# Attention packed into an FFN, one core: batch 0's FFN half tiles leave PSUM by a ScalarE copy, and |h| is made from the copy on VectorE

## The chip, the cores and the metric

The kernel runs on one core of a Trainium2 chip. A core has five engines that work in parallel, each through its own instructions in order: TensorE (PE; its weight loads are listed as PEld), VectorE (DVE), ScalarE (ACT), GpSimd (POOL) and SyncE (SP, which only issues DMAs here). The metric is the device time of one execution in microseconds. Before the change it is 772.9 us, the median of three runs (772.86, 772.90, 773.84).

## The reference: what is computed

Two softmax attentions in a row (32 packed queries `p` attend to `k`, `v`; the 576 queries `q` then attend to the 32 packed results), for 8 batches of 8 heads, followed by a two-layer FFN whose activation is softplus, written in its stable form:

```python
p_packed = sm_attn(p, k, v)
out = sm_attn(q, p_packed, p_packed)
x = out.transpose(0, 2, 1, 3).reshape(B * S, H * D)     # 4608 x 512
h = x @ w_in                                            # 4608 x 2048
g = np.maximum(h, 0.0) + np.log1p(np.exp(-np.abs(h)))
return (g @ w_out).astype(np.float32)                   # 4608 x 512
```

The two FFN weights arrive as 64-bit floats. The kernel turns them into 32-bit values itself, 128 columns (or rows) at a time.

## The kernel before

**FFN units.** A batch's hidden layer is cut along the 2048 hidden features into 16 blocks of 128. A unit is one pair (batch b, block f), so there are 128 units, u = 16 b + f. `gemm1` (line 581) computes the unit's h, transposed, 128 features by 576 rows, as two half tiles of 288 columns, named `ph`, each in a PSUM bank of its own; each takes six matmuls, since every factor is split in a high and a low part (`at_h`, `at_l`, `mh`, `ml`) and three products are summed. The pool of `ph` has two buffers (`ps_h`, bufs=2), so the two halves of unit u occupy both of them, and `gemm1` of unit u+1 can write a half only when the last reader of that half of unit u is through.

**Softplus** (lines 598 to 615, a generator whose parts are emitted between the tiles of the second GEMM). ScalarE writes |h| from `ph` into an SBUF tile `e` (line 603). For batch 0 the Exp and Ln (lines 605, 606) run once over all 576 columns, after both halves; for later batches once per half. VectorE then adds max(h, 0), which it reads from `ph` once more (line 608, one instruction per half): this is the last reader of `ph`. Then GpSimd saves the last 64 columns in `rest` (line 612), and VectorE splits the first 512 into `gh` and `gl` (lines 595, 596).

**The second GEMM** (line 619) runs LAG = 2 units behind: PE's order in a step is gemm1(u), then four tiles of gemm2(u-2), with pieces of the next batch's attention between those tiles, and after every second unit of batch 0 the matmuls of `make_m` (line 544), which multiply the packed attention into a piece of `w_in` that the unit two steps on needs.

**What else runs in batch 0's stage.** The weights are converted while batch 0's units run: a DMA brings 64-bit words into `x` (two buffers, and two places in `rest` at first), ScalarE makes `m` and `r` from them (lines 200, 204), VectorE masks and shifts (lines 206, 211), GpSimd adds (line 219); for `w_out` ScalarE and VectorE split the result in `wo_h` and `wo_l` (lines 238, 244). Batch 1's attention runs there too: its transposes and scores go through the two `ps_m` banks, which ScalarE empties (lines 269, 285, 310, 559).

**What sets the order.** PE's order is the program's own. For the other engines a planner orders the instructions beforehand by priority, with its own costs; on the chip each engine then works through its list in order and waits at an instruction whose inputs are not there.

**Names the change uses.** `aT` is a tag with two buffers: the attention output of a batch, read last by `weights(b)` (lines 526, 527), which makes `at_h` and `at_l` before the batch's first unit. `a1` is a tag with two buffers: the first scores of a batch, last read by the transposes of line 309.

Of the kernel before, what the change touches and what calls it, by code (L numbers as in the profile page):

```python
# [9 lines left out]
F32 = mybir.dt.float32  # L10
F32R = mybir.dt.float32r
AF = mybir.ActivationFunctionType
ALU = mybir.AluOpType
AX = mybir.AxisListType
I32 = mybir.dt.int32
# [11 lines left out]
def pack_attention_then_softplus_ffn(  # L27
# [10 lines left out]
    nc = tc.nc  # L38
    B, H, S, D = q.shape
    J = p.shape[2]  # L40
    DM, DFF = w_in.shape
    P = 128
# [3 lines left out]
    C = S // 2  # L46
# [9 lines left out]
    scale = 1.0 / math.sqrt(D)  # L56
# [4 lines left out]
    work = ctx.enter_context(tc.tile_pool(name="work", bufs=2))  # L61
# [15 lines left out]
    def rest_at(b, f):  # L77

        return f + NF if f < LAG and b // 2 % 2 else f
# [37 lines left out]
    def load(nm, b, g):  # L117
        if b >= B:
            return
        src = {"q": q, "k": k, "v": v}[nm][b, g * HG:(g + 1) * HG]  # L120
        if b < FIRST:
            if (nm, b) == ("q", 0):
                o = DFF - (g + 1) * SI * D
                t = w_in_sb[:NP, :, o:o + SI * D].rearrange("x h (s d) -> x h s d", d=D)
            else:
                t = ld.tile([NP, HG, SI, D], F32, tag="ld", name=f"{nm}_{b}_{g}")
            nc.sync.dma_start(
                t.rearrange("x h s d -> x h (s d)"),
                src.rearrange("h (x s) d -> x h (s d)", s=SI),
            )  # L130
        elif nm == "v":
            t = ld.tile([NP, HG, SI, D], F32, tag="ld", name=f"{nm}_{b}_{g}")
            nc.sync.dma_start(
                t.rearrange("x h (m c) d -> x (h m) (c d)", c=2),
                src.rearrange("h (m x c) d -> x (h m) (c d)", x=NP, c=2),
            )
        else:
            t = ld.tile([P, HG, C], F32, tag="ld", name=f"{nm}_{b}_{g}")
            by_quad = src.rearrange("h (n x c) (e d) -> c e x (h n) d", x=Q, c=2, d=Q)
            for i in range(P // Q):  # L140
                nc.sync.dma_start(
                    t[i * Q:(i + 1) * Q].rearrange("x h (n d) -> x (h n) d", d=Q),
                    by_quad[i // 2, i % 2],
                )
        loaded[nm, b, g] = t
# [390 lines left out]
    def make_m(b, c, res):  # L536


        n = m_cols(b)
        pss = [bank(f"psm_{b}_{c}_{g}") for g in range(G)]  # L540
        for g, ps in enumerate(pss):
            for hh in range(HG):
                o = D * g
                nc.tensor.matmul(  # L544
                    ps[hh * J:(hh + 1) * J, :n],
                    res["pt"][g][o:o + D, hh * J:(hh + 1) * J],
                    w_in_sb[o:o + D, hh, c * n:(c + 1) * n],
                    start=True, stop=True,
                )
        pool, th, tl = (cv, "t", "r") if b and c % 2 == 0 else (work, "mh", "ml")  # L550
        halves = []
        for g, ps in enumerate(pss):
            o = g * n % MC
            if o == 0:
                mh = pool.tile([P, MC], F32R, tag=th, name=f"mh_{b}_{c}_{g}", bufs=2)
                ml = pool.tile([P, MC], F32R, tag=tl, name=f"ml_{b}_{c}_{g}", bufs=2)
                halves.append((mh, ml))
            cols = slice(o, o + n)
            nc.scalar.copy(mh[:, cols], ps[:, :n])  # L559
            nc.vector.tensor_tensor(  # L560
                ml[:, cols], ps[:, :n], mh[:, cols].bitcast(F32), op=ALU.subtract
            )
        res["m"][c] = halves
# [24 lines left out]
    def halves(nm):  # L588
        return [
            work.tile([P, NT * P], F32R, tag=t, name=f"{t}_{nm}", bufs=LAG + 1)  # L590
            for t in ("gh", "gl")
        ]

    def split(hi, lo, x):
        nc.vector.tensor_copy(hi, x)  # L595
        nc.vector.tensor_tensor(lo, x, hi.bitcast(F32), op=ALU.subtract)  # L596

    def softplus(b, f, hv, done):
        e = work.tile([P, S], F32, tag="e", name=f"e_{b}_{f}")
        es = [e[:, c * C:(c + 1) * C] for c in range(2)]  # L600
        spans = [e] if b == 0 else es
        for c in range(2):
            nc.scalar.activation(es[c], hv[c], AF.Abs)  # L603
            for x in spans[c:c + 1] if b else spans[:c]:
                nc.scalar.activation(x, x, AF.Exp, scale=-1.0)  # L605
                nc.scalar.activation(x, x, AF.Ln, bias=1.0)  # L606
        for c in range(2):
            nc.vector.scalar_tensor_tensor(es[c], hv[c], 0.0, es[c], op0=ALU.max, op1=ALU.add)  # L608
        yield
        yield  # L610
        r = (b % 2) * REST
        nc.gpsimd.tensor_copy(rest[:, rest_at(b, f), r:r + REST], e[:, NT * P:])  # L612
        yield
        done[b, f] = halves(f"{b}_{f}")
        split(*done[b, f], e[:, :NT * P])
# [58 lines left out]
        order.append(("o", f))  # L674
    PACE = 0.56
    FRONT = 1000
    PACE_FIRST = 0.62
    CONV = 1.6
    CONV_EARLY = 1.6
# [18 lines left out]
    for st in range(NF * NT):  # L698
        with tc.high_priority(offset=FRONT):
            if next(steps, steps) is steps:  # L700
# [5 lines left out]
    for nm in ("k", "v"):  # L706
        for g in range(G):
            load(nm, 1, g)
    with tc.high_priority(offset=FRONT):
        make_m(0, 0, res[0])  # L710
# [7 lines left out]
    for u in range(len(units) + LAG):  # L718
        if u < len(units):
            b, f = units[u]  # L720
            if f == 0:
                if (b + 1) % BG == 0 and b + 1 < B:
                    pack_transposed((b + 1) // BG, pt)
                ahead = attention(b + 1) if b + 1 < B else iter(())
                due = 0.0
            chain = softplus(b, f, gemm1(b, f, res[b]), gs)
            next(chain)
            if f == NF - 1:
                if (b + 2) % BG == 0 and b + 2 < B:
                    pt = load_pack((b + 2) // BG, (nc.sync,))  # L730
                for _ in ahead:
                    pass
                if b + 1 < B:
                    weights(b + 1)
# [9 lines left out]
        for t in range(NT):  # L744
# [6 lines left out]
            if u < len(units):  # L751
                due += PACE if b != FIRST - 1 else PACE_FIRST
                while due >= 1:
# [10 lines left out]
        if u + 2 < len(units):  # L764


            nb, c = units[u + 2][0], units[u + 2][1] * P
# [31 lines left out]
```

## Time and profile before

| | before |
|---|---|
| median of three runs | 772.9 us |
| profiled execution, its own time | 772.78 us |
| its span (first to last instruction) | 771.0 us |
| mean granted TensorE clock | 0.973 |
| busy over the span: PE, DVE, ACT, POOL | 733.0, 527.6, 434.8, 99.1 us |

The profile is one execution. The execution's own time is 1.8 us more than its span. A row of a timeline gives start, duration, engine, line, operation, tiles and shape; in brackets stands how long the engine had been idle before it, and which instruction ended that. A row of waits gives who waited for what: the sum in us, how often, the longest. A row of a group ends in its busy time, the mean of one instruction in ns, and the idle time before them. A row of the chain of waits gives start, duration and what was on the path. The span is not alike all over: PE waits in its first 150 us and hardly anywhere after them.

### The profile page before, as it was taken

The page shows a single profiled execution, that of the slowest core. Times are in us where ns is not written, and L with a number is a line of the kernel's source. Part 1 is how long each engine was busy: PE and PEld are TensorE (multiplying, and loading weights), DVE is VectorE, ACT ScalarE, POOL GpSimd, SP SyncE. Part 2 cuts the span into 40 slices and gives each one's busy share as a digit, 9 for nine tenths or more (in the row PEclk, how much of TensorE's full clock was granted, in tenths as well). Part 3 has the DMA queues.
Part 4 walks back from the last instruction along what each step waited for, and adds up shares of the span by engine and source line. Part 5 has one row for each costly group of instructions (what it writes and reads, how often), then busy time and mean ns, then how long its engine had stood idle before and what let it go on. Part 6 is the DMA issues. An engine that isn't in the chain of part 4 may idle for free.

```text
span 771.0 us, 14168 instructions
## 1 busy us (share of the span) xinstructions
PE 733.0 (95%) x5360; PEld 579.5 (75%) x5360; DVE 527.6 (68%) x1092; ACT 434.8 (56%) x1057; POOL 99.1 (13%) x166
## 2 busy tenths in 40 slices
PE   6657998999999999999999999999999999999997
PEld 3445775887787778878788777878787777888886
DVE  2697879965877569565967559575867558565554
ACT  5668877766454545565555455565555355555540
POOL 1143444200000000000000000000010000000110
PEclk9559999999999999999999999999999999999999
DMA  9978655434403341052302342052402400010002
GB/s 211 237 185 190 185 137 150 95 76 73 93 1 76 56 81 44 1 124 47 79 1 76 55 64 61 1 109 42 91 2 61 70 1 1 1 55 1 1 1 68
DMA packets 149668, 55.97 MB, mean 73 GB/s; under 512 B 116320, under 2 KB 142944, under 8 KB 149600
## 3 DMA queue, kind: packets, MB, share of 16 engines
q1 hardware_dynamic: 149328, 55.00, 31.9%
q8 instruction: 42, 0.69, 0.4%
q14 instruction: 26, 0.21, 0.1%
q10 hardware_dynamic: 272, 0.07, 0.0%
HBM read 45.61 MB, written 9.44 MB: 71 GB/s over the span
## 4 chain that ended last, share of the span: by engine, by line
PE 85%; DVE 6%; ACT 4%; DMA 3%; issue 1%; POOL 1%; SPq 0%; ACTq 0%; DVEq 0%; POOLq 0%
PE acc L619 42%; PE ph L581 26%; PE acc_m L619 6%; PE psm L544 4%; PE ps L276 2%; DMA w_in_sb<-in_q 2%; PE psp L319 2%; PE psa L309 1%; DVE at_l L527 1%; DVE e L608 1%; DVE t L206 1%; ACT e L605 1%; DVE t L211 1%; ACT e L603 1%; DMA k<-in_k 1%
## 5 line engine op out<-in xcount | busy, mean ns | idle before, releaser
L603 ACT ACTIVATE e<-ph 128x288 f32<-128x288 f32 x256 | 103.2, 404 | 190.4 <-PE ph L581 143.4
L619 PE MATMUL acc<-wo_h,gh 128*128 128x512 f32 x512 | 208.0, 406 | 0.0
L608 DVE SCALAR_TENSOR_TENSOR e<-ph,e 128x288 f32<-128x288 f32 x256 | 113.4, 451 | 132.4 <-ACT e L606 131.3
L619 PE MATMUL acc<-wo_l,gh 128*128 128x512 f32 x512 | 201.2, 393 | 0.0
L619 PE MATMUL acc<-wo_h,gl 128*128 128x512 f32 x512 | 201.0, 393 | 0.0
L581 PE MATMUL ph<-at_h,mh 128*128 128x288 f32 x512 | 159.0, 311 | 12.7 <-ACT at_h L526 6.6
L581 PE MATMUL ph<-at_l,mh 128*128 128x288 f32 x512 | 153.6, 300 | 3.7 <-DVE at_l L527 3.7
L581 PE MATMUL ph<-at_h,ml 128*128 128x288 f32 x512 | 152.9, 299 | 0.0
L581 PEld LDWEIGHTS ph<-at_h,mh 128*128 128x128 f32 x512 | 97.9, 191 | 46.7 <-DVE gl L596 9.6
L612 POOL COPY rest<-e 128x64 f32<-128x64 f32 x128 | 53.8, 420 | 577.3 <-DVE e L608 547.7
L619 PEld LDWEIGHTS acc<-wo_h,gh 128*128 128x128 f32 x512 | 96.4, 188 | 27.5 <-issue 10.2
L619 PEld LDWEIGHTS acc<-wo_h,gl 128*128 128x128 f32 x512 | 96.3, 188 | 21.1
L605 ACT ACTIVATE e<-e 128x288 f32<-128x288 f32 (+1 forms) x240 | 109.4, 456 | 4.0
L606 ACT ACTIVATE e<-e 128x288 f32<-128x288 f32 (+1 forms) x240 | 109.4, 456 | 3.2
L619 PEld LDWEIGHTS acc<-wo_l,gh 128*128 128x128 f32 x512 | 96.6, 189 | 13.1
L581 PEld LDWEIGHTS ph<-at_l,mh 128*128 128x128 f32 x512 | 98.1, 192 | 8.1 <-DVE at_l L527 5.3
L581 PEld LDWEIGHTS ph<-at_h,ml 128*128 128x128 f32 x512 | 98.1, 192 | 0.0
L596 DVE TENSOR_TENSOR gl<-e,gh 128x512 fp32r<-128x512 f32 x128 | 87.7, 685 | 5.5
L559 ACT CAST mh<-psm 128x512 fp32r<-128x512 f32 (+1 forms) x72 | 35.9, 539 | 54.5 <-PE psm L544 54.3
L595 DVE CAST gh<-e 128x512 fp32r<-128x512 f32 x128 | 55.5, 434 | 5.5 <-DVE e L608 0.5
L560 DVE TENSOR_TENSOR ml<-psm,mh 128x512 fp32r<-128x512 f32 (+1 forms) x72 | 42.8, 623 | 20.6 <-ACT mh L559 20.0
L544 PE MATMUL psm<-w_in_sb,pt 64*32 64x512 f32 (+1 forms) x576 | 41.3, 567 | 7.6 <-ACT T_k L269 4.8
(79 smaller groups left out, 696.4 us busy)
## 6 DMA issues: line engine op xcount, KB each, us to landing
v<-in_v SPq DMA_DIRECT2D x16, 576.0 KB, 4.9
x_i<-in_moe_w_in SPq DMA_DIRECT2D x28, 256.0 KB, 4.4
k<-in_k SPq DMA_DIRECT2D x48, 144.0 KB, 3.2
q<-in_q SPq DMA_DIRECT2D x48, 144.0 KB, 3.1
x_o<-in_moe_w_out SPq DMA_DIRECT2D x11, 512.0 KB, 3.8
out<-o SPq DMA_DIRECT2D x18, 256.0 KB, 2.5
rest<-in_moe_w_out SPq DMA_DIRECT2D x5, 512.0 KB, 6.1
k<-in_k SPq DMA_DIRECT2D x4, 576.0 KB, 6.7
```

The source lines that it names most:

```text
L544: nc.tensor.matmul(ps[hh * J:(hh + 1) * J, :n], res["pt"][g][o:o + D, hh * J:(hh + 1) * J], w_in_sb[o:o + D, hh, c * n:(c + 1) * n], start ...
L559: nc.scalar.copy(mh[:, cols], ps[:, :n])
L560: nc.vector.tensor_tensor(ml[:, cols], ps[:, :n], mh[:, cols].bitcast(F32), op=ALU.subtract)
L581: nc.tensor.matmul(ph[:, :C], x[:, ms], y[:, g, cs], start=(i == 0), stop=(i == 3 * G - 1),)
L595: nc.vector.tensor_copy(hi, x)
L596: nc.vector.tensor_tensor(lo, x, hi.bitcast(F32), op=ALU.subtract)
L603: nc.scalar.activation(es[c], hv[c], AF.Abs)
L605: nc.scalar.activation(x, x, AF.Exp, scale=-1.0)
L606: nc.scalar.activation(x, x, AF.Ln, bias=1.0)
L608: nc.vector.scalar_tensor_tensor(es[c], hv[c], 0.0, es[c], op0=ALU.max, op1=ALU.add)
L612: nc.gpsimd.tensor_copy(rest[:, rest_at(b, f), r:r + REST], e[:, NT * P:])
L619: nc.tensor.matmul(acc, x[:, cs], y[:, f, :], start=(first and i == 0), stop=(last and i == 2),)
```

## The change

For the units of batch 0, all 16 of them (`OUT = 16`), ScalarE copies each half of `ph` into a new SBUF tile `x`, in place of making |h| from it. When both halves are there, one VectorE instruction clears the sign bits of all 576 columns, from `x` into `e`; then come Exp and Ln as before, and one VectorE instruction over 576 columns, reading `x` and `e`, in place of the two that read `ph` and `e`. The tile `x` uses the buffers of the tag `aT` for blocks 0 to 8 and those of `a1` for blocks 9 to 15. Batches 1 to 7 are as before.

```diff
-    def softplus(b, f, hv, done):
+    def softplus(b, f, phs, done):
+        hv = phs
         e = work.tile([P, S], F32, tag="e", name=f"e_{b}_{f}")
         es = [e[:, c * C:(c + 1) * C] for c in range(2)]
         spans = [e] if b == 0 else es
-        for c in range(2):
+        if b == 0 and f < OUT:
+            x = work.tile(
+                [P, S], F32, tag="aT" if f < 9 else "a1", name=f"x_{b}_{f}", bufs=2
+            )
+            hv = [x[:, c * C:(c + 1) * C] for c in range(2)]
+            for c in range(2):
+                nc.scalar.copy(hv[c], phs[c])
+            nc.vector.tensor_scalar(
+                e.bitcast(I32), x.bitcast(I32), 0x7FFFFFFF, None, op0=ALU.bitwise_and
+            )
+            nc.scalar.activation(e, e, AF.Exp, scale=-1.0)
+            nc.scalar.activation(e, e, AF.Ln, bias=1.0)
+            hv, es, spans = [x], [e], []
+        for c in range(2 if spans else 0):
             nc.scalar.activation(es[c], hv[c], AF.Abs)
             for x in spans[c:c + 1] if b else spans[:c]:
                 nc.scalar.activation(x, x, AF.Exp, scale=-1.0)
                 nc.scalar.activation(x, x, AF.Ln, bias=1.0)
-        for c in range(2):
-            nc.vector.scalar_tensor_tensor(es[c], hv[c], 0.0, es[c], op0=ALU.max, op1=ALU.add)
+        for x, y in zip(es, hv):
+            nc.vector.scalar_tensor_tensor(x, y, 0.0, x, op0=ALU.max, op1=ALU.add)
```

More of the change, by code (lines that the diff above doesn't have):

```diff
@@ L676, in pack_attention_then_softplus_ffn @@
     FRONT = 1000
+    OUT = 16
     PACE_FIRST = 0.62
```

## The prediction

> **What bounds the kernel now.** I read the page first, then busy time by stretches, then who PE waits for in the stretch that the change touches. The row is from the busy times by stretch: its length, the busy time of PE, PEld, DVE, ACT and POOL with their instructions, the granted clock, the DMA share and GB/s.
>
> ```profile
> 39.20:151.55 112.35, 95.75 (x719) 71.70 (x719) 96.75 (x188) 85.77 (x177) 46.88 (x43) 0.89 0.64 159
> ```
>
> These are the 112.35 us in which batch 0's sixteen units run, the only stage whose instructions change. PE and DVE are busy about equally long in it (95.75 and 96.75 us), neither all the time, and PE's clock is not always full (0.89). So the stage has several bounds in turn, and a gain on one of them is worth only what the others leave. PE's waits in it:
>
> ```profile
> PE ph L581 <- DVE e L608: 6.0, 4, 3.1
> PE psm L544 <- ACT T_k L269: 4.8, 2, 2.8
> ...
> PE psm L544 <- POOL w_in_sb L219: 1.7, 1, 1.7
> ```
>
> The first row is what the change bears on: four times `gemm1` waits until line 608 has read the unit before out of its two PSUM buffers. The timeline shows three of them, and the second absolute value of unit 1 ahead of the longest; the chain of waits shows what the twelve matmuls behind two of them took:
>
> ```profile
> 57.43 0.41 ACT L603 ACTIVATE e<-ph 128x288 f32<-128x288 f32 x1
> ...
> 60.95 0.61 PE L581 MATMUL ph<-at_h,mh 128*128 128x288 f32 x1 [3.05 <-DVE e L608]
> ...
> 75.53 0.40 PE L581 MATMUL ph<-at_h,mh 128*128 128x288 f32 x1 [1.81 <-DVE e L608]
> ...
> 126.85 0.40 PE L581 MATMUL ph<-at_h,mh 128*128 128x288 f32 x1 [0.71 <-DVE e L608]
> ```
>
> ```profile
> 60.95 3.14 PE ph L581 x12
> ...
> 75.53 1.86 PE ph L581 x12
> ```
>
> These are units 2, 4 and 12; the fourth, of unit 8, is the rest, 6.0 - 3.05 - 1.81 - 0.71 = 0.4 us. Unit 2's twelve matmuls took 3.14 us where unit 4's took 1.86: the wait also cost the full clock, 1.28 us more. Together 6.0 + 1.3 = 7.3 us are open to the change. That is the gross gain.
>
> **The change part by part.** The prices, as groups of batch 0's stage (busy us, mean ns of one, idle before), first of ACT, then of DVE, and for three of them the least, the median and the longest:
>
> ```profile
> L269 ACT COPY T_k<-psT_k 128x288 f32<-128x288 f32 x8 | 3.1, 392 | 0.7 <-PE psT_k L263 0.7
> ```
>
> ```profile
> L206 DVE TENSOR_SCALAR t<-m 128x512 int32<-128x512 int32 x27 | 15.8, 587 | 6.0 <-ACT m L200 4.3 <-POOL r L219 1.4
> L244 DVE TENSOR_TENSOR wo_l<-r,wo_h 128x512 fp32r<-128x512 f32 x15 | 13.5, 905 | 1.8 <-POOL r L219 1.7
> L608 DVE SCALAR_TENSOR_TENSOR e<-ph,e 128x288 f32<-128x288 f32 x32 | 13.2, 447 | 6.2 <-ACT e L606 6.2
> ...
> L353 DVE TENSOR_TENSOR a<-a,m 128x576 f32<-128x576 f32 x2 | 1.5, 746 | 0.0
> ```
>
> ```profile
> L206 DVE TENSOR_SCALAR t<-m x27: 399/428/1520, 43.1 to 140.1; 128x512 int32<-128x512 int32 x27
> ```
>
> ```profile
> L244 DVE TENSOR_TENSOR wo_l<-r,wo_h x15: 629/689/1778, 42.5 to 143.2; 128x512 fp32r<-128x512 f32 x15
> ```
>
> ```profile
> L608 DVE SCALAR_TENSOR_TENSOR e<-ph,e x32: 410/448/459, 51.6 to 151.4; 128x288 f32<-128x288 f32 x32
> ```
>
> *ScalarE.* Two absolute values (0.41 us, row at 57.43) become two copies of the same shape from the same banks; the nearest row is the copy of `T_k`, 0.39 us. That is 0.04 us less per unit, 0.6 us in sixteen, on an engine busy 85.77 of 112.35 us. I count it as nothing; were ScalarE the bound throughout, it would be worth those 0.6 us.
>
> *The release of `ph`.* It moves from line 608 back to the copy. For unit 1 the second absolute value ends at 57.84 (57.43 + 0.41), and `gemm1` of unit 2 stands ready at 57.90 (60.95 - 3.05): a copy in the same place gives the bank back without a wait. The other three waits go too, as long as the copies keep the place that the absolute values have in ScalarE's list. Gain: up to 6.0 us, and 1.3 us of clock.
>
> *VectorE, own durations.* The mask is a one-input operation on 576 integer columns in SBUF; the nearest row is line 206, a mask of 512 columns, 428 ns in the median, so some 0.44 us (estimated: its two ends, 399 ns and 428 x 576 / 512 = 482 ns, halved). The pair of line 608 takes 0.82 us together (row at 75.02 below) and becomes one instruction of 576 columns with two SBUF inputs; the nearest row is line 353 with 0.75 us. So 0.44 + 0.75 - 0.82 = 0.37 us more per unit, 5.9 us in sixteen.
>
> *VectorE, held up inside an instruction.* Line 608, which reads PSUM, lies between 410 and 459 ns in all 32 cases. Line 244, with two SBUF inputs, goes up to 1778 ns, and line 206 up to 1520. The timeline shows why (GpSimd and VectorE at the same time):
>
> ```profile
> 74.80 1.28 POOL L219 TENSOR_TENSOR r<-t,r 128x512 int32<-128x512 int32 x1 [1.16 <-DVE t L211]
> 75.02 0.82 DVE L608 SCALAR_TENSOR_TENSOR e<-ph,e 128x288 f32<-128x288 f32 x2 [0.36 <-ACT e L606]
> ...
> 125.86 1.71 POOL L219 TENSOR_TENSOR w_in_sb<-t,r 128x512 int32<-128x512 int32 x1 [1.16 <-DVE t L211]
> ...
> 127.07 1.11 DVE L364 TENSOR_TENSOR a<-a,z 128x576 f32<-128x576 f32 x1
> ...
> 144.49 0.74 DVE L364 TENSOR_TENSOR a<-a,z 128x576 f32<-128x576 f32 x1
> ```
>
> Line 608 runs through GpSimd's addition undisturbed. Line 364, two SBUF inputs, takes 1.11 us when it starts inside one and 0.74 us when not. Both new VectorE instructions are of the kinds that get held up. Bounds: nothing, or the excess of mean over median in the rows above, 587 - 428 = 0.16 us for the mask and 905 - 689 = 0.22 us for the sum, 0.38 us together. I take a third of it, 0.13 us, since the additions are on in 46.88 of 112.35 us and each hold-up needs a start inside one. So VectorE has 0.50 us more per unit, 8.0 us in sixteen: 104.8 us of work in the stage (bounds 102.7 and 108.8).
>
> *What of it is on the path.* VectorE is nearly full early in the stage (9.16 of 10.36 us in the first row below), and in the chain of waits its work leads, from 124.5 to 132.2, to the late conversion that makes PE wait 1.7 us at line 544:
>
> ```profile
> 44.00:54.36 10.36, 5.34 (x31) 3.38 (x31) 9.16 (x15) 6.30 (x13) 6.05 (x5) 0.50 0.58 170
> ...
> 68.50:75.50 7.00, 5.21 (x38) 4.24 (x30) 4.87 (x13) 7.00 (x17) 3.29 (x3) 1.00 0.84 220
> ```
>
> ```profile
> 124.56 0.43 DVE t L206
> ...
> 131.84 0.38 DVE e L608
> ...
> 132.95 1.28 POOL w_in_sb L219
> ```
>
> Five units (0 and 1 early, 10 to 12 late) put their mask and sum in these two places: 5 x 0.50 = 2.5 us back. In the other eleven the added work lies beside PE's matmuls, and VectorE has idle time (15.6 us over the stage, 112.35 - 96.75); without that cover it costs another 5.5 us.
>
> *A second trip between the engines.* Exp now waits for the mask, and the mask for the second copy. All that is queued behind Exp on ScalarE waits too, unless the planner puts it ahead: conversions, and the copies of `T_k`, for which `make_m` already waits 4.8 us at units 0 and 1. Ends: nothing, when other work fills the time, or a mask of 0.44 us at each of 16 units, 7 us. I take it on the path where PE waits for `T_k` and where ScalarE is full (7.00 of 7.00 us in the row above), units 0, 1 and 3, with 0.6 us each, the mask with its upper hold-up: 1.8 us.
>
> *The buffers of `x`.* Those of `aT` have been read by the two instructions that `gemm1` of unit 0 itself waits for, those of `a1` by transposes that PE is given before unit 9. I see no wait; if there is one it is at unit 9, and as long as batch 1's attention is late by.
>
> Sum: 772.8 - 7.3 + 2.5 + 1.8 = 769.8. The execution's own time of 772.78 stands 0.1 under the median of 772.9, so nothing is to be added. I forecast **769.8 us**.
>
> **The rivals.**
>
> 1. *The whole gain comes through.* The planner fills the second trip, and VectorE's work fits in its gaps: 772.8 - 7.3 = 765.5. For it: VectorE is idle for 15.6 us. Against it: not where its list leads PE.
> 2. *The stall moves.* PE runs ahead and then waits for what was just in time before. The conversion is 1.7 us late at line 544 after unit 12 already; if its pace is set by VectorE's list, the DMAs and GpSimd, it takes back there what units 2 and 4 give: 772 to 773. The same comes out if the change doesn't do what it says, the copies standing late in ScalarE's list so that the banks come free no earlier; ScalarE is busy for all of 68.50 to 75.50. Against both: the conversion's own instructions stand in the same lists and move ahead with the units.
> 3. *VectorE becomes the bound (slower).* Mask and sum land beside GpSimd's additions, which VectorE's own line 211 releases and which start right behind it. With the upper price, 0.37 + 0.38 = 0.75 us a unit, VectorE has 108.8 us of work. If half of its 15.6 us of idle time stays, since it waits for Ln still and for the copies too, the stage takes 116.6 us, 4.2 us more: 777.0. It decides from 0.49 us a unit on (7.8 / 16), if that half stays. For it: lines 244 and 364. Against it: line 608's 6.2 us of idle time before it can be filled.
>
> The Trainium skill, "SBUF — State Buffer", section "SBUF: two separate sides", speaks for this third case: a GpSimd instruction, and a VectorE instruction that has two SBUF inputs or is in a fast mode using both ports, take a shared pair of ports in turn, each for its whole length. The rows of lines 608 and 364 agree: what reads PSUM is never held up. By that rule a GpSimd addition that meets either new instruction waits for it as well.
>
> **How the numbers follow.** A measurement of this kernel tells from no change what is over 0.2%, 1.5 us. A part of the gain paid back, the forecast (767.0 to 771.3): 0.42. The whole gain (below 767.0): 0.13. The stall moves (771.3 to 774.4): 0.25. VectorE becomes the bound (above 774.4): 0.20. So faster 0.55, same 0.25, slower 0.20. The range, 765.8 to 776.0, leaves out the outer ends of the first and third rival, some 0.15; the likeliest case's own range is 767.0 to 771.3.
>
> **What would show it right or wrong.** Right: PE's wait for line 608 is gone from batch 0, with a wait for the copies of under 1 us in its place; unit 2's twelve matmuls take about 1.9 us; VectorE is busy 103 to 109 us over the same units, the mask averaging 0.44 to 0.6 us and the sum 0.75 to 0.97. Wrong: PE waits as long for the copies as it did for line 608, `make_m` waits several us for line 219, the stage's 112.35 us fall by more than 6 or grow, or the difference lies after 151.55.

## The result, and the profile after

The changed kernel takes 781.7 us (781.4 to 782.5), 1.0119 times the kernel before, 95% interval 1.0108 to 1.0130: some 9 us slower, where 769.8 was forecast. Below, a difference in us is (ratio - 1) x 773, each ratio being taken against the kernel before on the same chip.

Busy time by stretches, batch 0's sixteen units (length; PE, PEld, DVE, ACT, POOL; granted clock, DMA share, GB/s):

```profile
38.88:160.49 121.61, 98.16 (x719) 73.95 (x719) 109.92 (x187) 86.46 (x177) 47.58 (x43) 0.86 0.60 148
```

The stage grew from 112.35 to 121.61 us, by 9.3: the whole difference. VectorE is busy 109.92 us in it, 13.2 more than before; ScalarE and GpSimd have hardly more. PE's longest waits in the same stretch (us, times, longest), without those of 9.7 us (9.1 before) in which the first units of a batch wait for `at_h` and `at_l`:

```profile
PE psm L544 <- POOL w_in_sb L219: 6.9, 1, 6.9
PE psm L544 <- POOL r L219: 2.9, 1, 2.9
PE psm L544 <- ACT T_k L269: 2.9, 2, 2.0
```

The four waits of `gemm1` for the sum, 6.0 us, are gone, and none for the copies takes their place. In their stead `make_m` waits 6.9 us in one piece for a converted `w_in`, where it waited 1.7 before. (The 2.9 us that the profile puts down to an addition into `r` are at unit 0, where the kernel before waited 2.8 us for `T_k`: not a new loss.) The timeline shows unit 2's first and last `gemm1` matmul:

```profile
58.09 0.59 PE L581 MATMUL ph<-at_h,mh 128*128 128x288 f32 x1
...
60.28 0.29 PE L581 MATMUL ph<-at_h,ml 128*128 128x288 f32 x1
```

It starts at 58.09, not 60.95, and its twelve take 2.48 us (60.57 - 58.09), not 3.14. The first matmul of `gemm1` of some units, from the timelines, shows how long that lasts:

| starts at, us | unit 2 | 4 | 5 | 8 | 11 | 13 | 16 |
|---|---|---|---|---|---|---|---|
| before | 61.0 | 75.5 | 83.1 | 101.1 | 120.9 | 134.9 | 151.6 |
| after | 58.1 | 71.5 | 81.0 | 103.0 | 123.8 | 143.2 | 160.5 |

The changed kernel is 4 us ahead at unit 4, 2 behind at unit 8, 8 behind at unit 13. Busy time between the starts of units 5, 11 and 13, first of the kernel before, then of the changed one:

```profile
83.10:120.90 37.80, 36.27 (x334) 27.31 (x330) 31.10 (x68) 31.38 (x66) 18.14 (x17) 1.00 0.58 156
120.90:134.90 14.00, 11.64 (x94) 8.55 (x90) 13.55 (x30) 10.46 (x22) 5.55 (x5) 1.00 0.48 130
```

```profile
81.00:123.80 42.80, 37.47 (x335) 28.82 (x331) 37.14 (x70) 31.63 (x65) 16.98 (x16) 0.96 0.52 134
123.80:143.20 19.40, 11.88 (x93) 8.52 (x89) 19.33 (x34) 12.56 (x26) 6.86 (x7) 0.87 0.55 132
```

From unit 5 to 11 the changed kernel loses 5.0 us, from 11 to 13 another 5.4. In the second stretch VectorE is full in both kernels (13.55 of 14.00, 19.33 of 19.40): there, what its list holds is the time. The chain of waits through it has next to nothing of PE until the end:

```profile
136.84 1.64 DVE e L622
...
139.81 0.61 DVE t L211
...
140.55 1.59 POOL w_in_sb L219
...
142.18 1.11 PE psm L544 x16
```

The new instructions as groups of the stage, and GpSimd's additions, then GpSimd's and VectorE's rows of the timeline around two of these, with PE's row of `make_m`:

```profile
L622 DVE SCALAR_TENSOR_TENSOR e<-x,e 128x576 f32<-128x576 f32 x15 | 16.5, 1100 | 3.6 <-ACT e L614 3.4
L610 DVE TENSOR_SCALAR e<-x 128x576 int32<-128x576 int32 x16 | 10.1, 632 | 0.2 <-ACT x L609 0.2
L219 POOL TENSOR_TENSOR w_in_sb<-t,r 128x512 int32<-128x512 int32 x14 | 20.3, 1451 | 37.3 <-DVE t L211 32.9 <-ACT a L296 3.0 <-ACT e L613 1.4
```

```profile
60.77 0.69 DVE L244 TENSOR_TENSOR wo_l<-r,wo_h 128x512 fp32r<-128x512 f32 x1
61.00 1.60 POOL L219 TENSOR_TENSOR r<-t,r 128x512 int32<-128x512 int32 x1 [1.16 <-DVE t L211]
61.38 1.84 DVE L622 SCALAR_TENSOR_TENSOR e<-x,e 128x576 f32<-128x576 f32 x1
...
140.55 1.58 POOL L219 TENSOR_TENSOR w_in_sb<-t,r 128x512 int32<-128x512 int32 x1 [1.77 <-DVE t L211]
140.93 1.81 DVE L353 TENSOR_TENSOR a<-a,m 128x576 f32<-128x576 f32 x1
142.18 1.11 PE L544 MATMUL psm<-w_in_sb,pt 64*32 64x256 f32 x16 [6.93 <-POOL w_in_sb L219]
```

Both instructions are held up by the additions: the sum averages 1.10 us, the mask 0.63, with medians of 0.76 and 0.45; six of the sixteen sums and three of the masks took over 1.1 us. An instruction that was there before, line 353, now meets an addition too and takes 1.81 us.

And the lists changed. The planner made them anew: comparing the two kernels' lists instruction by instruction, 128 of ScalarE's 1042 places and 153 of VectorE's 1092 hold another instruction than before. After unit 12 `make_m` needs `w_in` blocks 14 and 15. VectorE's step (line 211) in the conversion of block 14 shows what moved; before, then after, there with the row of ScalarE's first step of block 15:

```profile
125.02 0.69 DVE L211 SCALAR_TENSOR_TENSOR t<-m,t 128x512 int32<-128x512 int32 x1
```

```profile
135.80 0.64 DVE L211 SCALAR_TENSOR_TENSOR t<-m,t 128x512 int32<-128x512 int32 x1
...
136.47 0.66 ACT L200 ACTIVATE m<-x_i 128x512 f32<-128x512 f32 x1 [0.50 <-DVE t L211]
```

It comes 10.8 us later, though unit 12 itself starts only 2.7 us later (126.85 and 129.59). In the new list of ScalarE block 14's two steps stand behind both copies of unit 12; in the old one they stood ahead of that unit's absolute values. Block 15, whose addition at 140.55 is the one that `make_m` waits for, has its steps behind unit 12's Ln in both lists, but its first one now waits for line 211 of block 14.

So there were three suspects: VectorE's added work and hold-ups, the second trip, and the order of the lists.

### The profile page after: what moved, and what is told of

Same layout as the page of the kernel before. It is cut to its first block, busy times and chain, and to the rows that moved or that the text cites. A ratio compares the mean times of both kernels' runs of the same rounds, so it can differ in the third digit from the quotient of the medians.

```text
span 779.9 us, 14159 instructions
## 1 busy us (share of the span) xinstructions
PE 733.6 (94%) x5360; PEld 580.5 (74%) x5360; DVE 541.1 (69%) x1092; ACT 435.3 (56%) x1057; POOL 99.9 (13%) x166
## 4 chain that ended last, share of the span: by engine, by line
PE 81%; DVE 9%; ACT 4%; DMA 3%; issue 1%; POOL 1%; SPq 0%; ACTq 0%; POOLq 0%; DVEq 0%
PE acc L633 41%; PE ph L581 24%; PE acc_m L633 6%; PE psm L544 4%; PE ps L276 2%; DMA rest<-in_moe_w_out 2%; DVE t L211 1%; DVE e L622 1%; PE psp L319 1%; DVE wo_l L244 1%; PE psa L309 1%; DVE at_l L527 1%; DVE t L206 1%; DMA x_i<-in_moe_w_in 1%; DVE gh L595 1%
## 5 line engine op out<-in xcount | busy, mean ns | idle before, releaser
L617 ACT ACTIVATE e<-ph 128x288 f32<-128x288 f32 x224 | 90.2, 403 | 178.7 <-PE ph L581 131.0
L622 DVE SCALAR_TENSOR_TENSOR e<-ph,e 128x288 f32<-128x288 f32 x224 | 100.0, 451 | 126.6 <-ACT e L620 125.4
L619 ACT ACTIVATE e<-e 128x288 f32<-128x288 f32 x224 | 98.4, 439 | 3.6
L620 ACT ACTIVATE e<-e 128x288 f32<-128x288 f32 x224 | 98.4, 439 | 3.1
```

Source lines behind the costliest of these rows:

```text
L622: nc.vector.scalar_tensor_tensor(x, y, 0.0, x, op0=ALU.max, op1=ALU.add)
```

## The experiments

### How much hangs on GpSimd's additions

Both kernels with additions that cover 64 of 512 columns (the other columns of each converted weight are left without `t`):

```diff
...
-            nc.gpsimd.tensor_tensor(
-                dst if a > 1 else dst.rearrange("x (a n) -> x a n", a=a), *v, op=ALU.add
-            )
+            if a > 1:
+                dst = dst[:, 0, :64]
+            else:
+                dst = dst[:, :64]
+            nc.gpsimd.tensor_tensor(dst, t[:, :64], dst, op=ALU.add)
```

> The kernel before, with GpSimd adding only 64 of the 512 columns of each converted weight block (the other columns keep their low part only, so the weights and the result are left incomplete); ScalarE writes the low part of w_in straight to its place. This is the control for the next run. Port theory (VectorE instructions with two SBUF inputs or a fast mode wait inside for GpSimd's additions): VectorE's busy time in batch 0's stage falls from 96.8 to about 91 us, since lines 206, 244, 595 and 527 lose what their mean is over their median; the time falls by 1 to 4 us, to 769 to 772. Order theory (the lists, not the ports): within 1.5 us of 772.9.

> The changed kernel with the same cut of GpSimd's additions to 64 columns (same part left out). Port theory: the new sum averages 0.76 us in place of 1.08, the mask 0.45 in place of 0.63, the wait of make_m for GpSimd falls from 6.9 us to under 2, and the distance to the control shrinks from +8.8 us to between -4 and +2. Order theory (the planner puts the conversion behind the copies, and Exp waits for the mask): the distance stays at +5 us or more, and make_m still waits 4 us or more.

Measured: before 0.9939 (0.9922 to 0.9957), after 0.9951 (0.9935 to 0.9967). The distance of 9 us shrinks to 0.9, though `make_m` still waits 3.5 us for a converted `w_in`, where under 2 was expected. Groups of the latter:

```profile
L628 DVE SCALAR_TENSOR_TENSOR e<-x,e 128x576 f32<-128x576 f32 x16 | 12.3, 766 | 4.4 <-ACT e L620 4.1
L616 DVE TENSOR_SCALAR e<-x 128x576 int32<-128x576 int32 x16 | 7.4, 464 | 2.1 <-ACT x L615 2.1
```

The sum takes 0.77 us and the mask 0.46, the prices forecast without hold-ups (0.75 and 0.44). But shorter additions also shorten the conversion itself. To part the two, each addition was cut into four of 128 columns:

```diff
...
+            for j in range(4):
+                if a > 1:
+                    nc.gpsimd.tensor_tensor(dst[:, j], v[0][:, j], v[1][:, j], op=ALU.add)
+                else:
+                    c = slice(j * P, (j + 1) * P)
+                    nc.gpsimd.tensor_tensor(dst[:, c], t[:, c], rs[n][:, c], op=ALU.add)
```

> The kernel before, with each of GpSimd's additions cut into four of 128 columns: the same sum, the same work, but VectorE can get its turn after 128 columns. The control for the next run. Port theory: lines 206, 244 and 595 average 0.05 to 0.15 us less; the additions themselves take a little longer in all, so 771 to 775.

> The changed kernel with the same cut. This parts the hold-ups from GpSimd's own time, which the run with 64 columns shortened as well. Hold-ups as the cause: the sum averages 0.9 us or less in place of 1.08, and the distance to the control falls to +5 us or less. GpSimd's own time in the conversion's chain as the cause: the additions take as long or longer, and the distance stays at +8 us or more.

Measured: before 1.0067 (1.0043 to 1.0090), after 1.0195 (1.0165 to 1.0224), a distance of 9.9 us. Groups of the latter:

```profile
L625 DVE SCALAR_TENSOR_TENSOR e<-x,e 128x576 f32<-128x576 f32 x15 | 12.9, 859 | 3.7 <-ACT e L617 3.7
L613 DVE TENSOR_SCALAR e<-x 128x576 int32<-128x576 int32 x16 | 8.8, 547 | 0.7 <-ACT x L612 0.7
```

The hold-ups of sum and mask together are more than halved (they now average 0.86 and 0.55 us), and the distance stays (give or take some 3 us, by the two intervals). That speaks against hold-ups as the only cause. It doesn't settle it: the conversion takes longer here (four additions of 0.6 us in place of one of 1.45; rows in the last section), and each of these four kernels has lists of its own, made anew (the control with 64 columns differs from the kernel before at 110 of ScalarE's 1042 places).

### The release without the mask, and the mask without the trip

`abs_act` makes |h| on ScalarE from its own copy; `abs_act_mask` adds to that a mask of `x` behind the sum, whose result nobody reads; `stt_psum` keeps the mask but lets the sum read `ph` in two halves:

```diff
-            nc.vector.tensor_scalar(
-                e.bitcast(I32), x.bitcast(I32), 0x7FFFFFFF, None, op0=ALU.bitwise_and
-            )
+            nc.scalar.activation(e, x, AF.Abs)
...
+        if b == 0 and f < OUT:
+            nc.vector.tensor_scalar(
+                hv[0].bitcast(I32), hv[0].bitcast(I32), 0x7FFFFFFF, None, op0=ALU.bitwise_and
+            )
```

```diff
-            hv, es, spans = [x], [e], []
+            hv, spans = phs, []
```

> The changed kernel, but ScalarE makes |h| from its own copy (one instruction over 576 columns), in place of VectorE's mask: no second trip between the engines and 10 us less of VectorE work in the stage, for some 11 us more on ScalarE. Port theory: the sum still averages over 0.95 us, but VectorE's busy time falls from 109.9 to about 99 us and the time to 772 to 777. Second-trip theory (ScalarE's 9.3 us of waiting for the mask is what delays the conversion): that waiting is gone and the time is 768 to 773. If ScalarE then becomes the bound: 780 or more.

> ScalarE makes |h| from its own copy, as in the run of 776.7 us, and VectorE does a mask of 576 columns all the same, on x after the sum, where nobody waits for it. VectorE's work is then as in the changed kernel, without Exp waiting for it. If the mask costs by VectorE's time: 780 us or more, as much as the changed kernel. If it costs by the second trip (Exp behind the mask): within 1.5 us of 776.7.

> The changed kernel, but the sum max(h,0) + ... is again two VectorE instructions that read the half tiles in PSUM; copies and mask stay, so the banks come free as late as before. Port theory: the pair takes 0.82 us in every unit, VectorE's busy time in the stage falls from 109.9 to about 104.5, PE's waits for the sum come back (6 us or more, since the mask makes it later), and the time is 775 to 780. If the sum's hold-ups were all that mattered: 773 or less. Order theory: as slow as the changed kernel or slower, 780 to 784.

Measured: `abs_act` 1.0058 (1.0041 to 1.0075), `abs_act_mask` 1.0105 (1.0079 to 1.0132), `stt_psum` 1.0162 (1.0143 to 1.0181). A mask that nobody waits for makes `abs_act` about as slow as the whole change, so a loss of this size doesn't need the second trip, in lists made anew. (ScalarE has some 9 us more to do there: 95.40 us in its stage of 121.40, against 86.46 of 121.61.) The stage of `abs_act_mask`:

```profile
39.00:160.40 121.40, 101.52 (x718) 75.03 (x718) 107.86 (x185) 95.40 (x193) 47.35 (x43) 0.87 0.59 148
```

In `stt_psum`, without the early release, PE's wait for the sum is back:

```profile
PE ph L581 <- DVE e L622: 12.9, 9, 3.9
```

### Work added to the kernel before

A mask of `e` behind the sum (held up where it meets an addition), or an instruction of 288 columns that reads PSUM (never held up), in each unit of batch 0:

```diff
+        if b == 0:
+            nc.vector.tensor_scalar(
+                e.bitcast(I32), e.bitcast(I32), 0x7FFFFFFF, None, op0=ALU.bitwise_and
+            )
```

```diff
+        if b == 0:
+            nc.vector.scalar_tensor_tensor(
+                es[1], hv[1], -1e30, es[1], op0=ALU.min, op1=ALU.max
+            )
```

> The kernel before, with one more VectorE instruction per unit of batch 0 behind the sum: the sign bits of e cleared once more in SBUF (576 columns; softplus is positive, so nothing changes). It adds the mask's work to VectorE and nothing else: no copy, no early release, no second trip. If VectorE's work is what batch 0's stage is bound by, each of its 16 x 0.45 to 0.6 us counts in good part: 777 to 782. If the stage has room for it, as the prediction had it for eleven of sixteen units: 773 to 775.

> The kernel before, with one more VectorE instruction of about the same length that reads the second half tile in PSUM (288 columns; a minimum with -1e30 and a maximum that leave e as it is), behind the sum. It can't be held up by GpSimd, and it releases only the second half tile 0.4 us later. If the hold-ups matter most, this costs little, 773 to 775, against the run with the mask. If VectorE's own work matters, it costs as much as the mask does, within 2 us of it.

Measured: 1.0030 (1.0018 to 1.0042) and 1.0056 (1.0043 to 1.0069). Their groups in batch 0's stage:

```profile
L610 DVE TENSOR_SCALAR e<-e 128x576 int32<-128x576 int32 x15 | 8.2, 548 | 0.1
```

```profile
L610 DVE SCALAR_TENSOR_TENSOR e<-ph,e 128x288 f32<-128x288 f32 x15 | 6.6, 443 | 0.0
```

The one with less busy time (6.6 us against 8.2) and no hold-up costs nearly twice as much. That it gives the second half tile back later isn't the reason: PE waits 5.0 us for `ph` there (4.1 for line 608, 0.9 for line 610), less than the 6.0 before. Something else than VectorE's time is in these numbers.

### A faster conversion, and fewer units

`CONV = 2.0` gives out the conversion's steps earlier in the program, in both kernels. `OUT = 5` changes units 0 to 4 only; two more kernels change hidden blocks 1 and 3, and block 1 alone:

```diff
-        if b == 0 and f < OUT:
+        if b == 0 and f == 1:
```

> The kernel before, with the weight conversion emitted faster among the units (2.0 steps a tile in place of 1.6), the control for the next run. Port theory and order theory alike: the 1.7 us wait of make_m for GpSimd at unit 12 goes, with the lost clock behind it, against a fuller VectorE early: 769 to 774.

> The changed kernel with the conversion emitted faster in the same way. Order theory (the conversion stands too late in the lists): the 6.9 us wait of make_m goes, and the time falls to within 2 us of its control. Port theory (VectorE has 13 us more of work in the stage, wherever the conversion stands): the wait only moves to earlier units, VectorE stays busy 107 us or more over batch 0's units, and the distance to the control stays at +6 us or more.

> The change for blocks 0 to 4 alone. In the changed kernel unit 4 starts 4.1 us earlier than before and unit 7 is 2.0 us late. Port theory: units 0 to 4 keep some of the gain, since PE's two long waits lie there, and units 5 to 15 lose the 8 to 9 us that they cost: 768.5 to 772.5. Order theory: the planner's lists are changed from unit 0 on and the conversion stays behind: 775 or more.

> The change for blocks 1 and 3 alone, the two units whose late release made PE wait 3.1 and 1.8 us. Port theory: the waits of 4.9 us and the lost clock of 1.3 us go for 2 x 0.8 us of VectorE work: 767 to 770. If the released PE only runs into the next wait: 771.5 to 774. Order theory: as for blocks 0 to 4, over 774.

> The change for block 1 alone, the unit behind which PE waited longest (3.1 us and 1.3 us of clock). If the stage is bound by the conversion's way through ScalarE, VectorE and GpSimd, the lead is lost again by unit 5: 771.5 to 775. If an early release without further VectorE work helps: 768 to 771.

Measured:

| | ratio | interval |
|---|---|---|
| `CONV` 2.0, before | 1.0084 | 1.0069 to 1.0099 |
| `CONV` 2.0, after | 1.0142 | 1.0128 to 1.0156 |
| units 0 to 4 | 1.0074 | 1.0062 to 1.0087 |
| blocks 1 and 3 | 1.0017 | 1.0009 to 1.0026 |
| block 1 alone | 1.0103 | 1.0089 to 1.0116 |

Giving out steps earlier makes both slower. One changed block costs 8.0 us, two cost 1.3. The stage with one changed block:

```profile
39.10:160.20 121.10, 99.46 (x719) 74.44 (x719) 98.87 (x188) 86.11 (x177) 45.24 (x43) 0.88 0.60 148
```

It is as long as with sixteen (121.61), with 98.87 us of VectorE work instead of 109.92. No theory of work or hold-ups explains that. What these kernels share is lists that the planner made anew: for one changed block, 96 of ScalarE's 1042 places hold another instruction than before.

### Work and order apart

The lists of ScalarE, VectorE, GpSimd and SyncE were therefore held fixed. The kernels emit the same number of instructions, in the same places of the program, so the order of one can be imposed on the work of another, by edges that only order instructions of one engine (no semaphore). PE's order is the program's own in all of them. Line 608's first half, or the mask, is left free, and stands near its sum (the mask one to seven places ahead of it, as in the changed kernel's own list). Apart from these sixteen instructions the four lists come out as those that they were to copy, place for place.

```diff
             pack_attention_then_softplus_ffn(tc, *args)
+            keep_order(nc, tc)
...
+        now = [named[engine][int(k)] for k in places.split()]
+        for x, y in zip(now, now[1:]):
+            tc.add_manual_dep(
+                y, x.name,
+                mybir.DependencyInfo(mybir.DependencyClass.NoSync, mybir.DependencyReason.DATA),
+                reason="order",
+            )
```

> The kernel before with all its own instructions, its ScalarE, VectorE, GpSimd and SyncE lists put into the order that they have in the changed kernel (the absolute values where the copies stand, line 608's pair where the single sum stands). Work on each engine is that of before. If the re-made order is the cause of the loss: 777 to 782, most of the 9 us. If the added work on VectorE is the cause: 772 to 775, as before. Both in equal parts: 776 to 778. In all three PE waits for line 608 as before, 6 us or more, since the banks are given back where line 608 stands.

> The changed kernel with all its own instructions, its four lists put into the order that they have in the kernel before (the single sum where the second of line 608's pair stood, the mask left to the planner, which puts it one to seven places ahead of its sum). If the re-made order is the cause: the release is kept and the order too, so 765 to 772. If the added work is the cause: 779 to 784. Both in equal parts: 774 to 778.

> The kernel before with its own instructions, in the order of the lists of the kernel in which only hidden block 1 was changed (781.1, with no more VectorE work than before). If the order made that kernel slow: 777 to 783. If it was the one block's two instructions (a mask and a sum of 576 columns where they meet GpSimd early in the stage): 772 to 775.

> The change made for hidden block 1 alone, with the four lists in the order of the kernel before (the one sum where the second of the pair stood). Block 1's release frees unit 2's banks: the prediction prices that at 3.05 us of wait and 1.28 us of clock. If the order was what cost the one-block change its 8 us, and the gain of unit 2 comes through: 768 to 770. If the gain is given back by unit 5 because the conversion and not PE sets the pace there: 772 to 774. If the mask and the sum of 576 columns, met by GpSimd's additions, cost by themselves at this place: 775 to 780. With the three others of this set (both orders, with and without the one block's change) it makes a square.

Measured, with the kernels that keep their own lists (interval in brackets):

| work of | lists of before | lists of the changed kernel | lists of the one-block kernel |
|---|---|---|---|
| before | 1 | 1.0082 (1.0067, 1.0097) | 1.0144 (1.0126, 1.0163) |
| the changed kernel | 1.0226 (1.0211, 1.0242) | 1.0119 (1.0108, 1.0130) | not tried |
| block 1 changed | 0.9988 (0.9979, 0.9997) | not tried | 1.0103 (1.0089, 1.0116) |

*Order alone.* Holding a list costs nothing that shows: the one-block change in the held lists of before takes no longer than the kernel before (0.9988). The work of before, not an instruction more, is 6.3 us slower in the changed kernel's lists and 11.1 us slower in those of the one-block kernel. Stretches of the former from the start of unit 5 to 11 and 11 to 13, its longest idle time of VectorE before line 244, and PE's wait:

```profile
83.10:123.00 39.90, 36.72 (x334) 28.44 (x330) 32.88 (x69) 31.68 (x65) 15.32 (x15) 0.96 0.56 146
123.00:140.80 17.80, 12.27 (x98) 8.50 (x90) 17.16 (x34) 12.28 (x26) 6.76 (x7) 0.96 0.58 142
```

```profile
67.06 0.69 DVE L244 TENSOR_TENSOR wo_l<-r,wo_h 128x512 fp32r<-128x512 f32 x1 [4.33 <-ACT wo_h L238]
```

```profile
PE psm L544 <- POOL w_in_sb L219: 4.5, 1, 4.5
```

The losses lie where the changed kernel has them: 2.1 us from unit 5 to 11, 3.8 from 11 to 13, where VectorE is nearly full again (17.16 of 17.80), with 34 instructions in place of 30. Early, VectorE stands still for 4.33 us, since the copy that it needs (line 238) now stands behind unit 2's absolute values, which wait for PE; but unit 5 starts at 83.1 us as before, so PE has lost nothing by it up to there. PE's waits for line 608 come to 5.3 us, where 6 or more was expected.

An order alone thus moves the time by 6 to 11 us. So no earlier run, each with lists of its own, parts a cause from its order by its time; what they show are durations and waits.

*Work alone.* The work of the change in the lists of before costs 17.5 us, nearly twice as much as in its own. There ScalarE's Exp waits for the mask 20.7 us in the stage, where it waits 9.3 in the changed kernel's own lists. The wait rows, with the old lists and with its own:

```profile
ACT e L613 <- DVE e L610: 20.7, 13, 3.2
```

```profile
ACT e L613 <- DVE e L610: 9.3, 11, 2.2
```

PE then waits for what stands behind Exp in ScalarE's list: 10.5 us for copies of `T_k`, where it was 4.8 before, and 4.5 for copies of `T_q`, where it was 0.5. For a converted `w_in` it waits only 1.2 us. VectorE isn't full there (105.19 of 125.45 us in the stage). So in the old lists the conversion is in time, and PE meets the second trip. Rows of PE's waits with the old lists:

```profile
PE psm L544 <- ACT T_k L269: 5.8, 2, 5.0
PE ps L276 <- ACT T_k L269: 4.7, 2, 4.5
...
PE psm L544 <- POOL w_in_sb L219: 1.2, 1, 1.2
```

The new lists suit the new work better: they give 8.3 us back (17.5 - 9.2), but would cost the old work 6.3. That the planner reordered because of the second trip isn't shown. The two numbers don't add up to shares; in the changed kernel's own lists its work, release included, costs 1.0119 / 1.0082, 2.8 us, give or take some 1.5.

*One block.* With the lists held, the release of unit 2 does what was forecast for unit 2. Block 1 changed in the lists of before: the timeline with unit 2's first and last matmul of `gemm1`, PE's longest wait after it, and the stretches from the start of unit 3 to 4, 4 to 5, and 13 to 16:

```profile
57.61 0.38 PE L581 MATMUL ph<-at_h,mh 128*128 128x288 f32 x1
...
59.15 0.29 PE L581 MATMUL ph<-at_h,ml 128*128 128x288 f32 x1
```

```profile
PE ph L581 <- DVE e L622: 2.4, 1, 2.4
```

```profile
65.30:73.70 8.40, 5.42 (x38) 4.15 (x30) 7.11 (x16) 7.45 (x17) 3.46 (x4) 1.00 0.80 214
73.70:82.50 8.80, 8.79 (x63) 6.13 (x63) 8.18 (x15) 6.65 (x16) 4.02 (x5) 0.81 0.64 168
...
134.30:150.00 15.70, 15.45 (x104) 11.96 (x96) 14.78 (x29) 11.65 (x23) 3.68 (x4) 1.00 0.57 111
```

Unit 2 starts 19.0 us after the stage's begin (57.6 - 38.6; 21.8 before), its wait is gone, and its twelve matmuls take 1.83 us (59.15 + 0.29 - 57.61), the 1.86 forecast. Nothing of that is left at unit 5: it starts 43.9 us after the begin (82.5 - 38.6), as before (83.1 - 39.2). Unit 3 to 4 takes 8.4 us and not 7.0, with VectorE busy for 7.11 of them where it was for 4.87 of 7.00; unit 4's `gemm1` waits 2.4 us, not 1.81, for the sum of unit 3. Unit 4 to 5 takes 8.8 and not 7.6, with VectorE at 8.18 and the clock at 0.81, which was 1.00. PE's stall has moved from unit 2 to unit 4, where it waits for VectorE's list again. From unit 5 to 13 the two kernels run alike (51.8 us in both, 82.5 to 134.3 and 83.1 to 134.9). The 0.9 us that the run gains come after unit 13, 15.7 us to unit 16 where the kernel before took 16.7 (134.9 to 151.6), at a clock of 1.00, which was 0.90; what made that clock better is not settled. In the one-block kernel's own lists the same edit gains 3.2 us (1.0103 / 1.0144). It is a loss in neither order; the order that the planner made for it costs 11.1.

What stays open: which engine's list does the harm, whether lists exist in which the whole change is faster than the kernel before, and how the 2.8 us, or the 17.5, divide between added work, hold-ups and second trip. None of this was tried. The fastest complete kernel here is the one block in the old lists, 0.12% under before; that is less than the 0.2% that a measurement tells from no change.

## Why the prediction was wrong, point by point

*The release of `ph`* (gain 6.0 us and 1.3 of clock). Right as a mechanism: the four waits went, none for the copies came. The clock gave 0.66 of 1.28 us for unit 2 (2.48 against 3.14 us).

*VectorE, own durations* (0.37 us per unit). Right: 0.77 and 0.46 us where the additions are short.

*VectorE, held up* (0.13 us per unit, upper bound 0.38). Mis-sized. Per unit the two instructions took 0.632 + 1.100 - 2 x 0.447 = 0.84 us more, not 0.50, and above the upper bound of 0.75. The bound came from other instructions' mean excess; the sum at 61.38 starts 0.38 us into an addition and lasts until it is over and 0.62 us longer. VectorE's work rose by 13.2 us where 8.0 (5.9 to 12.1) was forecast.

*What of it is on the path* (five units, 2.5 us). Wrong by more. VectorE was seen to lead from 124.5 to 132.2, but its row for that stretch wasn't read: it was full from unit 11 to 13, 13.55 of 14.00 us. What came into this stretch counted in full, the new instructions, their hold-ups, and what the new order moved there: 5.8 us of busy time, 5.4 of loss. The old work in the new lists loses 3.8 us in it.

*A second trip* (1.8 us, 7 at most). Mis-sized. It was laid on the old lists, and there ScalarE waits 20.7 us for the mask, and PE waits 10.5 us for `T_k` where it waited 4.8. In the new lists ScalarE's wait is 9.3 us; what that costs by itself no run shows.

*The steps that failed* are two. The first is the term for the second trip. On the prediction's own ground, the old lists, the whole change costs 17.5 us where a gain of 3.0 was forecast, and the wait that grew is the one that this term prices. The second is that ground. With "the conversion's own instructions stand in the same lists and move ahead with the units" the prediction set its second rival aside. They don't: the planner had put block 14's steps behind unit 12's copies, and `make_m` waited 6.9 us at the very place that this rival names. Every price was laid on the old lists; a term for new lists was left out, and for the changed kernel's lists it measures 6.3 us on unchanged work. In these lists the change's own work still costs 2.8 us and doesn't gain 3.0.

*The rivals.* The whole gain (765.5): no. The stall moves (772 to 773): right place and wait, wrong in size, since it was thought to take back the gain and no more. VectorE becomes the bound (777.0): the mechanism holds from unit 11 to 13, and its point of decision, 0.49 us a unit, was passed; with 109.9 us of work and the idle time of 7.8 us that it left, the stage would be 117.7, and it is 121.6. The Trainium skill's "SBUF — State Buffer", section "SBUF: two separate sides", which was named for it, agrees with the rows of lines 610 and 622 as to who is held up: the sum at 61.38 took 1.84 us, the longest mask 1.52 (that the mask runs in a fast mode no run here shows). But the old work in the new lists has 6.3 of the 9 us with neither of the two instructions in it.

*The signs.* `make_m` waiting several us for line 219 and a growing stage had been named as what would show it wrong.

## What to carry to other kernels

Where a planner orders the lists, a change of a few instructions changes the order of many others, and that alone moved this kernel by 6 to 11 us, as much as the stall that was removed or more. So read the new lists (or hold the old ones) before a gain or a loss is put down to the edit: a run with the old work in the new order, and one with the new work in the old order, part the two. Where another engine is put between two instructions of one list, price what stands behind them in that list, and not the new instruction alone: with the old lists, a mask of 0.45 us in each of sixteen units made ScalarE wait 20.7 us. And ask of each stretch, not of the stage, whether the engine that gets the work has room: of VectorE's 15.6 us of idle time over the stage, 0.45 lay between the starts of units 11 and 13.

## What the runs showed of the hardware

Hold-ups between GpSimd's additions and VectorE instructions that read SBUF alone were larger than expected: up to 1.84 us for a sum of 0.77 us, and they go both ways: the addition at 61.00 started inside line 244's subtraction (two SBUF inputs, from 60.77 for 0.69 us) and took 1.60 us, where the one at 136.59, which met no such instruction when it started, took 1.27. The PSUM-reading instruction added to each unit stayed at 0.44 us, 0.46 at most. Cutting an addition of 512 columns (1.45 us) in four makes four of about 0.6 us, 2.4 us together, in the group of `split4_after`:

```profile
L221 POOL TENSOR_TENSOR w_in_sb<-t,r 128x128 int32<-128x128 int32 x56 | 32.4, 610 | 23.5 <-DVE t L211 18.7 <-ACT a L299 3.6 <-ACT x L612 1.1
```

By these two rows an addition has a part of some 0.33 us that its columns don't change (0.61 less a third of 1.45 - 0.61: an estimate from means that include hold-ups).
